# A fused attention, routed-expert and feed-forward kernel: order of loads, first scores and the mask matmuls

## The chip, the core and the metric

The kernel runs on one core of one Trainium2 chip. The metric is the device time of one execution, in microseconds (us); the runs shown are three executions, of which the median counts. One further execution was recorded by the hardware profiler, and all rows of a profile below come from it.

## What is computed

The reference has three stages. The result of each is the input of the next.

```
scores = q k^T / 8, block-causal over blocks of 64      # 4 batches, 8 heads, 576 rows, 64 columns
x   = softmax(scores) v                                 # 2304 tokens x 512
keep = x @ w_skip > 0;  e = argmax(x @ w_gate)          # one of 8 experts for a token that is kept
x[keep] += gate * (relu(x @ w1[e]) @ w2[e])             # w1: 512 x 1024, w2: 1024 x 512 for each expert
h   = x @ w_in;  out = (max(h,0) + alpha*min(h,0)) @ w_out   # 2048 wide
```

The weights w_in and w_out arrive in a 64-bit form, which the kernel decodes on VectorE (DVE) into a high and a low part.

## The kernel before

**Attention.** Two heads make a pair, and there are 16 pairs, numbered p. Each goes through the steps `tr` (q and k are turned on TensorE, tiles psq and psk), `tr_tail` (the last 64 rows, tile pst), `sc` (scores, tile pss, five query blocks i in the order 4, 3, 2, 1, 0), `row_max`, `expo`, `ptr` (the exponentials are turned, tile pspt), `pv` (tile pso), `norm` and `xout`. A table `OFF` of step offsets gives the order in which the steps are recorded, so that one pair's steps mix with its neighbours', and a scheduler then sets each engine's order. q and k are split into high and low float32r parts, and a score is the sum of three products (`PARTS`). The mask is one more small matmul of a tile `top` (a one in two rows) with a tile `neg` (a large negative number), which stands behind the first of the three products (L239). Matmuls of a constant tile (`warm`, tile psw) keep TensorE busy at a few places, eight of them behind the first load.

**Loads.** SyncE (SP) issues nearly all DMAs. A load of 512 KB goes through `bulk`: the load number n waits until load n minus `DEPTH` has landed, and `DEPTH` is 2. This wait stands in SP's own row of instructions, so whatever is behind it waits too. Small DMAs of SP (the lists, the rows of x) are not in that chain but stand in the same row.

**Experts.** The first 32 tokens of each expert are worked on together: `s_x` turns the gathered rows, `s_one(e)` is the product with w1 (tile psh), `s_ht(e)` turns its result (tile hts), `s_two(e)` is the product with w2 (tile psy). `AHEAD` is 3, so `s_one` of experts 0 to 2 runs ahead of the loop over experts. What an expert has beyond 32 tokens is done in `extra(e)`, a block under a condition on a register (L794); with this input it is skipped for experts 0, 1, 5, 6 and 7 and taken for 2, 3 and 4. Where it is skipped, each engine jumps. `level0(e)` gathers rows for it by GpSimd (POOL), two experts ahead. Which rows these are stands in the lists `li`, which SP reads from DRAM after GpSimd has scattered them there (L496); `load_list` issues four reads. Weights lie in three sets of buffers, so `load_w(e + 3)` comes after expert e. The last four pieces of expert 2 (its w2) are loaded where the lists are read, behind them. `dec_in` decodes pieces of w_in (raw tile dr, three buffers) between the experts.

**From experts to feed-forward.** `first_decode` decodes the first two pieces of w_out into the tile xz. `first_window` loads the first 512 rows of x into xz (L890), turns them (L899), adds the last group's result by a product with a selection matrix (L902) and splits them into xs. Then the feed-forward loop (`g1`, `act`, `g2`) runs, during whose first sixteen steps the rest of w_out is decoded.

```
def bulk(out, in_, free_run=False):
    ins = nc.sync.dma_start(out=out, in_=in_).ins
    if not free_run:
        if len(chain) >= DEPTH:
            tc.add_manual_dep(ins, chain[-DEPTH].name, ...)
        chain.append(ins)

load_areg(4); s_x(0); sends[B - 1]()       # sends: the list scatters
for i in range(KX): load_list(i)
load_w(2, range(4, 8))
```

Of the kernel before, what the change touches and what calls it, by code (L numbers as in the profile page):

```python
# [32 lines left out]
DEPTH = 2  # L33
# [14 lines left out]
def tile_kernel(ctx: ExitStack, tc: tile.TileContext, q, k, v, w_skip, w_gate, w1, w2, w_in, w_out, alpha, out):  # L48
# [27 lines left out]
    chain = []  # L76

    def bulk(out, in_, free_run=False):
        ins = nc.sync.dma_start(out=out, in_=in_).ins
        if not free_run:  # L80
            if len(chain) >= DEPTH:
                tc.add_manual_dep(ins, chain[-DEPTH].name, mybir.DependencyInfo(mybir.DependencyClass.Sync, mybir.DependencyReason.DATA), reason="few large loads at a time")
            chain.append(ins)
# [63 lines left out]
    top = acst.tile([128, 128], F32R, name="top")  # L147
    nc.vector.memset(top.bitcast(F32), 0.0)
    for r in (0, 64):
        nc.vector.memset(top[r:r + 1, 0:64].bitcast(F32), 1.0)  # L150
    neg = acst.tile([128, 64], F32R, name="neg")
    nc.vector.memset(neg.bitcast(F32), NEG)
# [33 lines left out]
    def load(p, nm, src):  # L186
        b, h0 = p // NP, p % NP * 2
        a = ld.tile([128, 5, 2, D], F32, tag=nm + "r", name=nm + "r")
        for x in range(2):
            nc.sync.dma_start(out=a[:, 0:4, x, :], in_=src[b, h0 + x, 0:512, :].rearrange("(t p) d -> p t d", p=128))  # L190
        nc.sync.dma_start(out=a[0:64, 4], in_=src[b, h0:h0 + 2, 512:S, :].rearrange("h p d -> p h d"))
        st[p][nm + "r"] = a
# [5 lines left out]
    def tr(p, nm):  # L198
        ps = ps_m.tile([128, 512], F32, tag="m", name="ps" + nm)
        for t in range(4):  # L200
            nc.tensor.transpose(ps[:, t * 128:t * 128 + 128], tok4(p, nm, t), ident)
        for c in "hl":
            st[p][nm + c] = tp.tile([128, 512 if nm == "q" else S], F32R, tag=nm + c, name=nm + c)
        split_qk(nm, *(st[p][nm + c][:, 0:512] for c in "hl"), ps)
# [23 lines left out]
    def sc(p, i):  # L228
        d = st[p]
        ps = d["s", i] = ps_s.tile([128, 2, 512], F32, tag="s", name="pss")  # L230
        if i < 4:
            n = 128 * i + 128
            qc = slice(i * 128, i * 128 + 128)
            for k, (a, b) in enumerate(PARTS):
                for x, hs in enumerate(half):
                    nc.tensor.matmul(ps[:, x, 0:n], d[a][hs, qc], d[b][hs, 0:n], start=(k == 0), stop=(k == 2))  # L236
                if k == 0:
                    for x, hs in enumerate(half):
                        nc.tensor.matmul(ps[:, x, n - 64:n], top[hs], neg[hs], start=False, stop=False)  # L239
        else:  # L240
            for c, o in ((slice(0, 512), ps[:, 0]), (slice(512, S), ps[:, 1, 0:64])):
                for k, (a, b) in enumerate(PARTS):
                    nc.tensor.matmul(o, qd[p % 2][:, int(a == "ql")], d[b][:, c], start=(k == 0), stop=(k == 2))

    def row_max(p, i):
# [5 lines left out]
        else:  # L251
            m = sm.tile([128, 1], F32, tag="m4", name="m4", bufs=2)
            nc.vector.tensor_reduce(out=m, in_=ps.rearrange("p x c -> p (x c)")[:, 0:S], axis=AX.X, op=ALU.max, negate=True)
# [309 lines left out]
    start = {load: WARM}  # L563
# [103 lines left out]
    AHEAD = 3  # L667
# [39 lines left out]
    def s_ht(e):  # L707
        hT = mw.tile([128, 2, 128], F32, tag="hts", name="hts", bufs=1)
        trans(sh[e], hT)
        sh[e] = hT  # L710
# [115 lines left out]
    sends[B - 1]()  # L826
    for i in range(KX):
        load_list(i)
    load_w(2, range(4, 8))
# [14 lines left out]
    s_ht(0)  # L844
    xs = {}
# [41 lines left out]
    def first_window():  # L887
        xz = xzs[0]
        for t in range(4):
            nc.sync.dma_start(out=xz[:, t], in_=xd[t * 128:t * 128 + 128, :])  # L890
# [18 lines left out]
    for e in range(E):  # L909
# [9 lines left out]
        else:  # L919
# [3 lines left out]
            s_ht(e + 1)  # L923
# [144 lines left out]
```

## Time and profile before

| | us |
|---|---|
| median of 3 runs | 860.8 |
| lowest and highest | 858.63, 864.05 |
| profiled execution, its own time | 854.09 |
| span of the profiled execution (first to last instruction) | 852.5 |
| TensorE (PE) busy in the span | 799.0 |
| DVE busy in the span | 458.8 |
| ScalarE (ACT) busy | 299.3 |
| GpSimd (POOL) busy | 162.4 |

Times in rows are us from the span's start. PEld is TensorE's weight load, SPq the queue of SyncE. In a row of the timeline, the bracket gives how long the engine had been idle before it and what ended that. PEclk is the granted TensorE clock: 1.00 is 2.4 GHz, 0.50 is 1.2 GHz. A busy time is a modelled one for matmuls, and a row may merge several instructions (x8).

### The profile page before, as it was taken

The page shows a single profiled execution, that of the slowest core. Times are in us where ns is not written, and L with a number is a line of the kernel's source. Part 1 is how long each engine was busy: PE and PEld are TensorE (multiplying, and loading weights), DVE is VectorE, ACT ScalarE, POOL GpSimd, SP SyncE. Part 2 cuts the span into 40 slices and gives each one's busy share as a digit, 9 for nine tenths or more (in the row PEclk, how much of TensorE's full clock was granted, in tenths as well). Part 3 has the DMA queues.
Part 4 walks back from the last instruction along what each step waited for, and adds up shares of the span by engine and source line. Part 5 has one row for each costly group of instructions (what it writes and reads, how often), then busy time and mean ns, then how long its engine had stood idle before and what let it go on. Part 6 is the DMA issues. An engine that isn't in the chain of part 4 may idle for free.

```text
span 852.5 us, 14562 instructions
## 1 busy us (share of the span) xinstructions
PE 799.0 (94%) x5548; PEld 613.9 (72%) x5548; DVE 458.8 (54%) x951; ACT 299.3 (35%) x779; POOL 162.4 (19%) x204
## 2 busy tenths in 40 slices
PE   7999999999986899998599988999999999999998
PEld 4777777777753665765388666888888888888887
DVE  4576757667657167798579898323222332222232
ACT  3777676766641123112143433211111112111111
POOL 1000110110103122313012211321222212222132
PEclk7999999999998799999799999999999999999999
DMA  6765354464313777877723221100110001000100
GB/s 123 169 197 143 87 147 108 96 159 126 95 36 89 251 254 244 267 254 240 239 101 94 80 83 42 50 0 1 50 50 0 1 26 50 0 1 1 38 13 25
DMA packets 96378, 85.84 MB, mean 101 GB/s; under 512 B 68601, under 2 KB 73913, under 8 KB 96272
## 3 DMA queue, kind: packets, MB, share of 16 engines
q1 hardware_dynamic: 93776, 78.88, 32.1%
q0 software_dynamic: 2496, 5.61, 2.0%
q8 instruction: 59, 0.97, 0.5%
q14 instruction: 47, 0.39, 0.2%
HBM read 73.20 MB, written 11.71 MB: 100 GB/s over the span
## 4 chain that ended last, share of the span: by engine, by line
PE 47%; DVE 9%; DMA 4%; issue 2%; ACT 1%; SPq 0%; DVEq 0%; ACTq 0%
PE psf L970 18%; PE psa L1001 6%; PE psa L1002 6%; PE psa L1011 6%; PE psh L752 4%; PE psy L763 3%; DVE dt L640 2%; DMA w2t<-in_moe_w_dram 1%; DVE dr L644 1%; DVE dt L641 1%; DVE gt L983 1%; DMA w1t<-in_moe_w_dram 1%; PE psh L777 1%; DVE dr L642 1%; DVE dr L638 1%
## 5 line engine op out<-in xcount | busy, mean ns | idle before, releaser
L970 PE MATMUL psf<-xs,whi 128*128 128x512 f32 (+1 forms) x640 | 159.6, 371 | 0.7 <-ACT xs L856 0.7
L987 POOL TENSOR_TENSOR gl<-gt,gh 128x512 fp32r<-128x512 f32 (+1 forms) x80 | 96.0, 1200 | 322.9 <-ACT gh L986 190.5
L986 ACT ACTIVATE gh<-gt 128x512 fp32r<-128x512 f32 (+1 forms) x80 | 47.1, 589 | 264.5 <-PE psa L1002 144.7
L970 PEld LDWEIGHTS psf<-xs,whi 128*128 128x128 f32 x640 | 114.3, 188 | 25.4 <-ACT xs L856 0.9
L982 DVE TENSOR_SCALAR gu<-psf,alf 128x512 f32<-128x512 f32 (+1 forms) x64 | 43.7, 683 | 158.3 <-PE psf L970 158.0
L970 PE MATMUL psf<-xs,wlo 128*128 128x512 f32 (+1 forms) x320 | 80.1, 372 | 0.0
L267 ACT ACTIVATE pe<-pss,mx 128x512 f32<-128x512 f32 (+3 forms) x128 | 66.6, 524 | 14.2 <-DVE mx L250 11.8
L970 PEld LDWEIGHTS psf<-xs,wlo 128*128 128x128 f32 x320 | 56.6, 188 | 11.7
L1001 PE MATMUL psa<-whi,gh 128*128 128x512 f32 x144 | 57.3, 398 | 6.5 <-ACT gh L986 6.5
L250 DVE TENSOR_REDUCE mx<-pss 128x2 f32<-128x1024 f32 (+1 forms) x64 | 52.4, 819 | 19.9 <-PE pss L236 17.3
L275 ACT ACTIVATE pt<-pspt 128x512 f32<-128x512 f32 (+3 forms) x112 | 52.1, 488 | 29.4 <-PE pspt L301 28.7
L1001 PE MATMUL psa<-wkg,gh 128*128 128x512 f32 x144 | 57.2, 397 | 1.7 <-ACT gh L986 1.7
L983 DVE SCALAR_TENSOR_TENSOR gt<-psf,gu 128x512 f32<-128x512 f32 (+1 forms) x80 | 51.0, 637 | 13.9 <-POOL gl L987 8.1
L1002 PE MATMUL psa<-wlo,gh 128*128 128x512 f32 x144 | 56.3, 391 | 0.0
L1002 PE MATMUL psa<-wkg,gh 128*128 128x512 f32 x144 | 56.3, 391 | 0.0
L301 PE MATMUL pspt<-ident,pe 128*128 128x128 f32 x320 | 51.5, 287 | 0.1
L326 PE MATMUL pso<-pt,vr 128*64 128x256 f32 (+1 forms) x384 | 47.5, 352 | 2.3 <-ACT pt L275 2.1
L857 DVE TENSOR_TENSOR xs<-psx,xs 128x512 fp32r<-128x512 f32 x18 | 12.4, 692 | 60.4 <-ACT xs L856 60.4
L326 PEld LDWEIGHTS pso<-pt,vr 128*64 128x64 f32 x384 | 30.1, 136 | 16.9 <-ACT pt L275 7.2
L752 PEld LDWEIGHTS psh<-xT,w1t 128*128 128x128 f32 x320 | 39.5, 205 | 1.5 <-issue 1.0
L752 PE MATMUL psh<-xT,w1t 128*128 128x128 f32 x320 | 40.2, 290 | 0.0
L301 PEld LDWEIGHTS pspt<-ident,pe 128*128 128x128 f32 x320 | 33.8, 141 | 6.7 <-issue 2.2
(231 smaller groups left out, 1374.3 us busy)
## 6 DMA issues: line engine op xcount, KB each, us to landing
w1t<-in_moe_w_dram SPq DMA_DIRECT2D x32, 512.0 KB, 4.5
w2t<-in_moe_w_dram SPq DMA_DIRECT2D x32, 512.0 KB, 4.5
dr<-in_moe_w_in_dram SPq DMA_DIRECT2D x16, 512.0 KB, 5.1
dr<-in_moe_w_out_dram SPq DMA_DIRECT2D x16, 512.0 KB, 3.7
out_dram<-ob SPq DMA_DIRECT2D x18, 256.0 KB, 2.0
qr<-in_q_dram SPq DMA_DIRECT2D x32, 128.0 KB, 4.9
kr<-in_k_dram SPq DMA_DIRECT2D x32, 128.0 KB, 2.6
vr<-in_v_dram SPq DMA_DIRECT2D x32, 128.0 KB, 2.5
```

Source lines behind the costliest of these rows:

```text
L250: nc.vector.tensor_reduce(out=m, in_=ps[:, :, 0:128 * i + 128], axis=AX.X, op=ALU.max, negate=True)
L267: ins = nc.scalar.activation(out=pt[:, x, 0:n], in_=ps[:, x, 0:n], func=AF.Exp, bias=m[:, x:x + 1], scale=1.0, accum_out=d["sum"][:, x * 4 ...
L275: nc.scalar.activation(out=o, in_=a, func=AF.Copy)
L301: nc.tensor.transpose(ps[:, y, j, :], e[:, x, j * 128:j * 128 + 128], ident)
L326: nc.tensor.matmul(d["o"][hs, c0:c0 + n * 128], v5[:, j, x, :], pt[:, x, 2 * j:2 * j + n].rearrange("p n c -> p (n c)"), start=(j == 0), s ...
L752: nc.tensor.matmul(ps[:, f], w[:, kk, c:c + 128], self.xT[:, kk], start=(kk == 0), stop=(kk == 3))
L970: nc.tensor.matmul(ps[:, 0:n], wsp[f // 4 * 4 + kk][a][:, ws], c[:, kk, 0:n], start=(n0 == 0 and kk == 0), stop=(n0 == 2 and kk == 3))
L983: nc.vector.scalar_tensor_tensor(out=t[:, 0:n], in0=ps[:, 0:n], scalar=0.0, in1=u[:, 0:n], op0=ALU.max, op1=ALU.add)
L987: nc.gpsimd.tensor_tensor(out=lo[:, 0:n], in0=t[:, 0:n], in1=hi[:, 0:n].bitcast(F32), op=ALU.subtract)
L1001: nc.tensor.matmul(o, hi[:, ts], whi, start=(f == 0), stop=False)
L1002: nc.tensor.matmul(o, hi[:, ts], wlo, start=False, stop=False)
L1011: nc.tensor.matmul(acc[w, t], lo[:, t * 128:t * 128 + 128], whi, start=False, stop=False)
```

## The change

Eight edits are made at once.

1. `DEPTH` goes from 2 to 3: a 512 KB load waits for the third load before it, not the second.
2. The four w2 loads of expert 2 stand ahead of the four list reads. The first of them waits for the ACT copy that ends `s_x(0)` (`tied`, `last_exp`).
3. `AHEAD` goes from 3 to 2 and hts gets two buffers: `s_one(2)` moves from ahead of the loop into the turn of expert 1, `s_ht(1)` from the turn of expert 0 to ahead of the loop.
4. The rows of `first_window` (xz) are loaded by GpSimd's queue; the loads of w_out behind them stay on SP.
5. k of pair 0 is loaded by ACT's queue.
6. The q transposes of pair 1 wait for the first row maximum of pair 0 (`first`).
7. Five more warm-up matmuls are recorded behind `tr_tail(0)`.
8. `top` and `neg` are bfloat16, and the mask matmuls of a block stand behind its three products, as the last of the sum.

```
-DEPTH = 2
+DEPTH = 3
...
+            if tied[0]:
+                tc.add_manual_dep(ins, tied.pop().name, ..., reason="first rows ahead of the weights")
...
-    top = acst.tile([128, 128], F32R, name="top")
+    top = acst.tile([128, 128], BF16, name="top")
...
-    neg = acst.tile([128, 64], F32R, name="neg")
+    neg = acst.tile([128, 64], BF16, name="neg")
...
+        queue = nc.scalar if p == 0 and nm == "k" else nc.sync
...
-            nc.tensor.transpose(ps[:, t * 128:t * 128 + 128], tok4(p, nm, t), ident)
+            ins = nc.tensor.transpose(ps[:, t * 128:t * 128 + 128], tok4(p, nm, t), ident)
+            if p == 1 and nm == "q" and t == 0:
+                tc.add_manual_dep(ins.ins, st[0]["first"].name, ..., reason="first scores first")
...
-                    nc.tensor.matmul(ps[:, x, 0:n], d[a][hs, qc], d[b][hs, 0:n], start=(k == 0), stop=(k == 2))
-                if k == 0:
-                    for x, hs in enumerate(half):
-                        nc.tensor.matmul(ps[:, x, n - 64:n], top[hs], neg[hs], start=False, stop=False)
+                    nc.tensor.matmul(ps[:, x, 0:n], d[a][hs, qc], d[b][hs, 0:n], start=(k == 0), stop=False)
+            for x, hs in enumerate(half):
+                nc.tensor.matmul(ps[:, x, n - 64:n], top[hs], neg[hs], start=False, stop=True)
...
-    start = {load: WARM}
+    start = {load: WARM, tr_tail: 5}
...
-    AHEAD = 3
+    AHEAD = 2
...
-        hT = mw.tile([128, 2, 128], F32, tag="hts", name="hts", bufs=1)
+        hT = mw.tile([128, 2, 128], F32, tag="hts", name="hts", bufs=2)
...
+    tied[0] = last_exp[0]
+    load_w(2, range(4, 8))
     for i in range(KX):
         load_list(i)
-    load_w(2, range(4, 8))
...
     s_ht(0)
+    s_ht(1)
...
-            nc.sync.dma_start(out=xz[:, t], in_=xd[t * 128:t * 128 + 128, :])
+            nc.gpsimd.dma_start(out=xz[:, t], in_=xd[t * 128:t * 128 + 128, :])
...
-            s_ht(e + 1)
+            if e + 1 < AHEAD - 1:
+                s_ht(e + 2)
+            elif e + 1 >= AHEAD:
+                s_ht(e + 1)
```

TensorE at the start of the program, before. psq with qr is here the turned q of pair 1; pss with qd is the scores of pair 0's block 4, pss with kh and qh those of its block 3.

```order
L221 MATMUL pst<-ident,qr 128x64
L221 MATMUL pst<-ident,kr 128x64
L201 MATMUL psq<-ident,qr 128x128 x4
L243 MATMUL pss<-kh,qd_168 128x512
L243 MATMUL pss<-kl,qd_168 128x512
L236 MATMUL pss<-kh,qh 128x512 x2
L243 MATMUL pss<-kh,qd_168 128x512
L243 MATMUL pss<-kh,qd_168 128x64
L239 MATMUL pss<-neg,top 128x64
```

The same place after the change, from the last products of block 4 on.

```order
L249 MATMUL pss<-kh,qd_168 128x64
L249 MATMUL pss<-kl,qd_168 128x64
L249 MATMUL pss<-kh,qd_168 128x64
L243 MATMUL pss<-kh,qh 128x512 x2
L243 MATMUL pss<-kl,qh 128x512 x2
L243 MATMUL pss<-kh,ql 128x512 x2
L245 LDWEIGHTS top
L245 MATMUL pss<-neg,top 128x64
L245 LDWEIGHTS top
L245 MATMUL pss<-neg,top 128x64
L206 MATMUL psq<-ident,qr 128x128 x4
L292 MATMUL pspt<-ident,p_267 128x128 x4
```

The q transposes of pair 1 stood ahead of the first scores and now stand behind two whole blocks of them; the mask matmuls of block 3 stood inside the sum and now end it. All thirteen warm-up matmuls stand ahead of the first transposes, the five new ones too.

SP where the experts begin, before (li are the lists, w2t the w2 of expert 2).

```order
L679 TENSOR_LOAD cnt
L679 ISA x2
L672 DMA li<-lst 128x8x2 x4
L79 DMA w2t<-in_moe_w_dram 128x2x512 x4
L679 TENSOR_LOAD cnt
L679 ISA x2
```

SP at the same place after the change.

```order
L685 TENSOR_LOAD cnt
L685 ISA x2
L80 DMA w2t<-in_moe_w_dram 128x2x512 x4
L678 DMA li<-lst 128x8x2 x4
L685 TENSOR_LOAD cnt
L685 ISA x2
```

The four weight loads and the four list reads have changed places.

SP at the end of the experts, before (L794 is the end of the last condition, xz the rows of the first window, dr raw pieces of w_out).

```order
L804 UNCONDITIONAL_BRANCH
L794 UNCONDITIONAL_BRANCH
L890 DMA xz<-xd 128x512 x4
L79 DMA dr<-in_moe_w_out_dram 128x1024 x3
L950 DMA xw<-xd 128x512 x4
```

POOL at the same place after the change.

```order
L810 UNCONDITIONAL_BRANCH
L800 ISA
L800 UNCONDITIONAL_BRANCH
L898 DMA xz<-xd 128x512 x4
L736 TENSOR_TENSOR yo<-ys,xgs 128x512
L598 DMA xd<-yo,sid 2305x512
```

The four reads of xz have left SP's row, where the loads of w_out now follow the last branch directly, and stand in POOL's row behind the last branch and ahead of the last group's sum and scatter.

## Rows read from the trace of the kernel before

**Rows 1.** Busy time by stage: PE, PEld, DVE, ACT, POOL, then PEclk, DMA share, GB/s
```profile
12.00:246.00 234.00, 231.04 (x2151) 169.05 (x2151) 148.90 (x418) 161.99 (x502) 18.74 (x39) 0.98 0.51 127
...
392.00:432.00 40.00, 25.67 (x414) 19.72 (x410) 26.96 (x48) 9.59 (x28) 8.37 (x9) 0.83 0.69 221
432.00:532.00 100.00, 91.79 (x395) 72.27 (x396) 89.31 (x148) 39.31 (x68) 21.05 (x15) 1.00 0.24 79
```
**Rows 2.** Timeline of PE, start of pairs 0, 1, 2: start us, us, instruction, idle
```profile
1.26 3.59 PE L62 MATMUL psw<-ones 128*128 128x512 bf16 x8 [1.26 <-DVE ones L128]
...
6.12 0.63 PE L201 MATMUL psk<-ident,kr 128*128 128x128 f32 x4 [0.41 <-DMA kr<-in_k_dram]
...
9.64 1.09 PE L201 MATMUL psq<-ident,qr 128*128 128x128 f32 x4 [2.62 <-DMA qr<-in_q_dram]
11.75 0.77 PE L243 MATMUL pss<-kh,qd 128*128 128x512 f32 x1 [1.02 <-ACT qd L212]
...
28.24 0.48 PE L243 MATMUL pss<-kh,qd 128*128 128x512 f32 x1
...
41.86 0.48 PE L243 MATMUL pss<-kh,qd 128*128 128x512 f32 x1
```
**Rows 3.** Busy time and PEclk in single microseconds near the start
```profile
9.00:10.00 1.00, 0.36 (x2) 0.39 (x3) 0.00 (x0) 0.00 (x0) 0.00 (x0) 0.63 0.45 103
...
22.00:23.00 1.00, 1.00 (x8) 0.88 (x8) 0.27 (x1) 0.34 (x3) 0.00 (x0) 0.54 1.33 226
```
**Rows 4.** Timeline of PE: a mask matmul, and a run of short bf16 matmuls
```profile
43.59 0.19 PE L239 MATMUL pss<-neg,top 64*128 64x64 f32 x2
43.62 0.47 PE L236 MATMUL pss<-kl,qh 64*128 64x512 f32 x2
...
251.01 0.24 PE L445 MATMUL psl<-ohb,ones 128*128 128x32 bf16 x4 [0.78 <-DVE ohb L437]
251.11 0.18 PE L446 MATMUL psl<-ohb,tri 128*128 128x40 bf16 x1
```
**Rows 5.** Timeline of SP, PE and POOL from 268 to 285 us
```profile
268.05 3.10 SPq L672 DMA_DIRECT2D li<-lst  x4
268.28 1.95 PE L719 MATMUL psy<-w2t,hts 128*32 128x128 f32 x34 [1.96 <-PEq L794]
...
271.26 7.18 SPq L79 DMA_DIRECT2D w2t<-in_moe_w_dram  x4
...
279.99 0.09 POOL L65 MEMSET pad<- 1x1 f32 x1 [6.14 <-DMA xg<-xd,li]
...
280.86 3.21 PE L719 MATMUL psy<-w2t,hts 128*32 128x128 f32 x56 [4.47 <-issue]
...
284.94 1.46 PE L687 MATMUL pst<-ident,xg 128*128 128x128 f32 x4 [0.25 <-DMA xg<-xd,li]
```
**Rows 6.** Timeline of SP, POOL, DVE and PE from 391 to 427 us
```profile
391.15 6.60 SPq L79 DMA_DIRECT2D w1t<-in_moe_w_dram  x4
...
407.24 0.96 POOL L589 DMA_INDIRECT xg<-xd,li  x1 [0.77 <-POOL pad L65]
...
410.33 5.32 SPq L79 DMA_DIRECT2D dr<-in_moe_w_out_dram  x3
...
415.36 0.43 DVE L637 TENSOR_SCALAR xz<-dr 128x512 int32<-128x512 int32 x1 [7.08 <-PE psy L719]
...
419.89 1.75 SPq L890 DMA_DIRECT2D xz<-xd  x4
...
422.74 4.01 PE L899 MATMUL psx<-ident,xz 128*128 128x128 f32 x16 [3.70 <-DMA xz<-xd]
...
424.62 0.48 DVE L728 TENSOR_SCALAR ys<-ys,gat 128x512 f32<-128x512 f32 x1
...
426.54 4.96 PE L902 MATMUL psx<-xz,ys 128*128 128x128 f32 x32
```
**Rows 7.** GpSimd's gathers (L589): time from issue to landing
```profile
DMA to landing us min/median/max: 3.4/5.6/7.2
```

More of the change, by code (lines that the diff above doesn't have):

```diff
@@ L76, in tile_kernel @@
     chain = []
+    tied = [None]
     def bulk(out, in_, free_run=False):
@@ L80, in bulk @@
         if not free_run:
+            if tied[0]:
+                tc.add_manual_dep(ins, tied.pop().name, mybir.DependencyInfo(mybir.DependencyClass.Sync, mybir.DependencyReason.DATA), reason="first rows ahead of the weights")
+                tied.append(None)
             if len(chain) >= DEPTH:
@@ L146, in tile_kernel @@
     nc.vector.tensor_scalar(out=tlo, in0=tok, scalar1=63, scalar2=None, op0=ALU.bitwise_and)
-    top = acst.tile([128, 128], F32R, name="top")
-    nc.vector.memset(top.bitcast(F32), 0.0)
+    top = acst.tile([128, 128], BF16, name="top")
+    nc.vector.memset(top, 0.0)
     for r in (0, 64):
-        nc.vector.memset(top[r:r + 1, 0:64].bitcast(F32), 1.0)
-    neg = acst.tile([128, 64], F32R, name="neg")
-    nc.vector.memset(neg.bitcast(F32), NEG)
+        nc.vector.memset(top[r:r + 1, 0:64], 1.0)
+    neg = acst.tile([128, 64], BF16, name="neg")
+    nc.vector.memset(neg, NEG)
     thi = acst.tile([128, 5], F32, name="thi")
@@ L188, in load @@
         a = ld.tile([128, 5, 2, D], F32, tag=nm + "r", name=nm + "r")
+        queue = nc.scalar if p == 0 and nm == "k" else nc.sync
         for x in range(2):
-            nc.sync.dma_start(out=a[:, 0:4, x, :], in_=src[b, h0 + x, 0:512, :].rearrange("(t p) d -> p t d", p=128))
-        nc.sync.dma_start(out=a[0:64, 4], in_=src[b, h0:h0 + 2, 512:S, :].rearrange("h p d -> p h d"))
+            queue.dma_start(out=a[:, 0:4, x, :], in_=src[b, h0 + x, 0:512, :].rearrange("(t p) d -> p t d", p=128))
+        queue.dma_start(out=a[0:64, 4], in_=src[b, h0:h0 + 2, 512:S, :].rearrange("h p d -> p h d"))
         st[p][nm + "r"] = a
@@ L200, in tr @@
         for t in range(4):
-            nc.tensor.transpose(ps[:, t * 128:t * 128 + 128], tok4(p, nm, t), ident)
+            ins = nc.tensor.transpose(ps[:, t * 128:t * 128 + 128], tok4(p, nm, t), ident)
+            if p == 1 and nm == "q" and t == 0:
+                tc.add_manual_dep(ins.ins, st[0]["first"].name, mybir.DependencyInfo(mybir.DependencyClass.Sync, mybir.DependencyReason.DATA), reason="first scores first")
         for c in "hl":
@@ L252, in row_max @@
             m = sm.tile([128, 1], F32, tag="m4", name="m4", bufs=2)
-            nc.vector.tensor_reduce(out=m, in_=ps.rearrange("p x c -> p (x c)")[:, 0:S], axis=AX.X, op=ALU.max, negate=True)
+            d["first"] = nc.vector.tensor_reduce(out=m, in_=ps.rearrange("p x c -> p (x c)")[:, 0:S], axis=AX.X, op=ALU.max, negate=True).ins
         d["m", i] = m
```

## The prediction

> **What bounds the kernel now.** I read the busy shares by stage first, then the timeline of the engine that is full in each stage, then the idle times in the stages where none is full.
>
> Attention, from 12 to 246 us, keeps PE busy for 231.0 of 234 us [rows 1]: only less work on PE, or work at a better clock, shortens it. One pair takes 41.86 − 28.24 = 13.62 us there. The first took 28.24 − 11.75 = 16.49 [rows 2]. The clock explains that: PE idles 2.62 us ahead of the transposes of pair 1 at 9.64, PEclk is 0.63 from 9 to 10 us and still 0.54 from 22 to 23 [rows 2, 3], so most of pair 0 runs near 1.2 GHz instead of 2.4.
>
> Between 392 and 432 us no engine is full: PE has 25.7 us of 40, DVE 27.0, and PEclk is 0.83 [rows 1]. The weights of the last expert come first, then three pieces dr of w_out; SP is held by these until 410.33 + 5.32 = 415.65, and its reads of xz go out only at 419.89. DVE waits 7.08 us for the first piece, PE 3.70 us for xz [rows 6]. From 432 to 532 us DVE is the fuller engine, 89.3 us against 91.8 of PE with its modelled ends [rows 1]; this stage starts when the first window is ready, so an earlier window moves everything behind it. The trace thus offers two places: the first pair and the end of the experts.
>
> **The start (edits 5, 6, 7).** Eight warm-up matmuls take 3.59 us, some of it before their pace settles: 0.43 to 0.45 each. Five more cost 5 × 0.43 = 2.1 us at that pace and half of it, 1.1, at the full clock; I take 1.7. They end at 1.26 + 3.4 + 1.7 = 6.35, where psk started at 6.12, after a wait of 0.41 for k [rows 2]. So ACT's queue for k is worth nothing alone: the warm-up covers k's landing with it or without it. Transposes psk take 0.63, psq of pair 0 as much and the last rows little: about 7.5. Scores came 1.02 us behind the last transposes because of ACT's copies [rows 2]; I allow 1.25, as k's and q's copies are now closer together. That gives the first scores at 8.75 instead of 11.75: −3.0.
>
> The 2.62 us wait for q of pair 1 disappears, for it now stands behind the scores of two blocks. The wait that replaces it, for the first row maximum, has queued behind it on PE only what follows those two blocks, and that has some 4 us of scores as cover; if DVE is late there, it costs a few tenths. What is idle is 1.25 us rather than 2.62, so I expect the clock to stay at 2.4 GHz. Pair 0 then takes somewhat less than 13.62, since no earlier pair's values are mixed into it, and some waits for copies remain: 13.0 against 16.49, −3.5. Together −6.5. If the clock falls all the same, only the −3.0 is left; if the added gaps are longer, it could be zero.
>
> **The mask (edit 8).** There are 64 blocks with two mask matmuls each. Before, the product that follows starts 0.03 us after the two [rows 4]; free of cost after the edit that is 64 × 0.03 = 1.9 us gained. A short bf16 matmul starts 0.10 / 4 = 0.025 us behind another [rows 4]: 128 × 0.025 = 3.2, and against 1.9 that is 1.3 lost. I take 0, in the middle; the row maximum waits for two tiny matmuls more, beside PE's next block.
>
> **Expert 2's weights and the lists (edits 2, 3).** SP issued the list reads at 268.05 for 3.10 us and the w2 loads from 271.26 to 278.44. Expert 2's extra part starts at 284.94 on the landing of its gathered rows, not of w2 [rows 5]. Its w2 is wanted only later, so loading it earlier buys nothing at first; the lists behind four loads of which the fourth waits for the first to land may come up to 4 us later, and with them the gathers. On the other side the loads behind move forward by some of the 7 us. s_one(2) only changes place (1.9 us of matmuls like those at 268.28), s_ht(1) too. I take 0 with −4 and +4 as ends.
>
> **Three loads (edit 1) and xz by GpSimd (edit 4).** From the first w1 issue at 391.15 to the end of the last dr issue at 415.65 stand eleven loads: 24.5 / 10 = 2.45 us each with two in flight [rows 6]. If latency sets the pace, three give two thirds, 1.63; if bandwidth sets it, 2.45 stays (the mean there is 221 GB/s, DMA share 0.69 [rows 1]). I take 1.9. The first dr goes out at 391.15 + 8 × 1.9 = 406.4, lands about 5.5 later (it took 415.36 − 410.33 = 5.0) and is decoded from 412 instead of 415.36. DVE's step L728 behind the decodes comes at 424.62 − 3.4 = 421.3.
>
> The xz reads on POOL wait for its gather at 407.24 (0.96 to issue) to land, 5.6 at the median and 7.2 at most [rows 6, 7], and for two joins of branches: 416. Four issues at the gather's 0.96 bring 420; the last lands some 3 us later, 423, at about the time at which L899 can follow. PE's L902 then starts near 423 instead of 426.54 [rows 6]: −3.5. Less time at half clock gives about 1.5 back, crowding of the DMA engines takes about 1: −4. If the bandwidth bounds and POOL is slow: 0 to +3. If all loads land at 1.63 and PE never slows: −8. In the stretch before, from 304 to 392, a faster stream buys nothing, since the next weights wait for buffers that PE's work frees; the last expert's w1 starts at 391 for that reason.
>
> The row shows DVE decoding in operations of 0.43 us just when POOL would issue. The Trainium skill, "SBUF — State Buffer", section "SBUF: two separate sides", says that a DMA issued from GpSimd has its descriptors written by GpSimd, which is locked out while DVE runs an operation in a 2-port mode. By that rule the xz reads would be late; no row here shows a GpSimd DMA beside decodes. It is the second rival below.
>
> **The sum.** −6.5 + 0 + 0 − 4 = −10.5. The profiled execution took 854.1 (span 852.5 and 1.6 around it), which gives 843.6. The median of the runs is 860.8, 6.7 above it; a time that is compared with this median has to carry this difference, so 860.8 − 10.5 = 850.3, and I predict 850.
>
> **Rivals.** All are given on the median.
>
> *The clock falls anyway.* Thirteen warm-up matmuls, then a gap of 1.25 us and small pieces: PEclk fell to 0.63 behind a gap of 2.62 [rows 2, 3], and nothing shows what 1.25 does. Then the start gives −3, the end −4: 853.8. Chance 0.17.
>
> *GpSimd is late with xz.* DVE's decodes hold the descriptors back. By rows, each of four issues can wait at most for one 0.43 us operation at a time and the stage gains nothing at its end: −6.5 and 0, 854.3. Against it: the gathers of the same queue land in 5.6 us beside DVE work. Chance 0.13.
>
> *Skipped branches get dearer (slower).* Five experts skip their extra part, and each time PE waits for its own instructions to come. The wait at 268.28, before the w2 loads went out, was 1.96; the one at 280.86, with two of them in flight, 4.47 [rows 5]: 2.5 more. If a third load in flight does such a thing at all five branches, 5 × 2.5 = 12.5 are lost. With the start's −6.5 and nothing at the end, this is +6, 867. It decides from 10.5 / 5 = 2.1 us for a branch on. Against it: the later skips already have two loads beside them, and the third adds less than the first two. Chance 0.14; half of it ends above 869.4.
>
> The Trainium skill, "Runtime: NRT & Kernel Launch", section "Instruction fetch mechanics", states that a taken branch to an instruction outside the fetched window forces a DMA fetch before execution goes on. The two waits of 1.96 and 4.47 fit this; that the load beside it lengthens it is this trace's reading alone.
>
> *The earlier weights hold the lists back.* The change puts w2 ahead, but the lists, and with them all gathers, come later, up to 5 us along expert 2's chain, which is bound by the landing of its rows [rows 5]: 855.3. Chance 0.08.
>
> **How the numbers follow.** The forecast has 0.48 (843 to 853 by itself). A measurement of this kernel tells about 1% from no change. Faster than 852.2: 0.46 from the forecast, a third of the first two rivals (0.10): 0.56. Slower than 869.4: half the third rival and 0.02 from chains not seen: 0.09. The rest, 0.35, is within 1%. The range 842 to 864 takes in all but the third rival's upper part and ends below the forecast by the −8 of the last stage and the −1.9 of the mask not adding up together.
>
> **What would show it.** Right: PEclk near 1 from 9 to 23 us, the first scores at 8.75, pair 1's scores about 6.5 us earlier; dr's first decode and L728 some 3.4 us earlier than their places, measured from the last expert's w1 issue; xz landed before PE asks for it. Wrong: PEclk near 0.5 behind the first scores; idle times behind L794's joins over 4 us at each skipped expert; lists later than 271 measured from `s_x(0)`; xz landing behind the decodes, with PE waiting there as before; loads still 2.4 us apart.

## The result and the profile after

Four executions of the changed kernel took 847.12 to 851.27 us, 849.84 at the median, beside 860.59 for four of the kernel before: ratio 0.9893, 95% interval 0.9858 to 0.9928 (an estimate of its own from the executions; the quotient of the two medians is 0.9875). A second comparison later (ten executions against 28) gave 0.9917, 0.9896 to 0.9938. So it is faster by about 1%, 7 to 9 us. Each ratio further below compares a run with executions of the kernel before made beside it, whose medians were 856.1 to 859.7. The execution in the profile took 848.45 us (span 846.9). The recorded one of before took 854.09, so the two traces differ by only 5.6; where the rest is comes out below.

Line numbers in this table are those of the changed kernel.

| milestone on PE, us | before | after | difference |
|---|---|---|---|
| first scores of pair 0 | 11.75 | 9.40 | -2.35 |
| first scores of pair 1 | 28.24 | 21.45 | -6.8 |
| first scores of pair 2 | 41.86 | 35.02 | -6.8 |
| end of attention: first of the last ten products with the gate weights (L416) | 247.19 | 238.62 | -8.6 |
| experts' first rows (L693) | 258.27 | 249.71 | -8.6 |
| gathered rows of expert 2 (L693) | 284.94 | 277.77 | -7.2 |
| first product behind the taken experts (L709) | 392.77 | 387.42 | -5.35 |
| s_two of the last expert (L725) | 417.09 | 414.12 | -3.0 |
| selection product of the first window (L910) | 426.54 | 422.38 | -4.2 |
| first product of feed-forward (L981) | 432.19 | 426.80 | -5.4 |

8.6 us are gained up to 250, 5.6 of them are gone at 414, and 2.4 come back by 427. From there on nothing changes.

Busy time by stage after, which answers to [rows 1] (PE, PEld, DVE, ACT, POOL, then PEclk, DMA share, GB/s):

```profile
12.00:246.00 234.00, 226.35 (x2201) 166.35 (x2201) 153.59 (x446) 163.16 (x513) 19.88 (x41) 1.00 0.51 127
...
392.00:432.00 40.00, 26.22 (x330) 20.77 (x331) 16.55 (x34) 10.23 (x27) 7.35 (x11) 0.87 0.54 183
432.00:532.00 100.00, 92.04 (x397) 72.38 (x396) 87.33 (x143) 38.63 (x66) 23.24 (x17) 1.00 0.25 79
```

Attention ends 8.6 us sooner, so PE's sum in the first row has some of the next stage's idle time in it. Between 392 and 432 PE is no fuller than before. DVE is down from 26.96 to 16.55 us there, but this is work that moved: the last decodes of w_in ended at 379.9 and not at 408.3, and from 246 to 304 us, where DMA moved 236 GB/s in place of 157, DVE was busy for 36.03 us in place of 27.13. Behind 379.9 DVE stood idle for 24.42 us, until w_out's first piece landed (below).

The start, timeline of PE after, which answers to [rows 2] (start us, us, instruction, idle before it):

```profile
1.26 5.27 PE L62 MATMUL psw<-ones 128*128 128x512 bf16 x13 [1.26 <-DVE ones L132]
6.37 0.60 PE L206 MATMUL psq<-ident,qr 128*128 128x128 f32 x4
6.80 0.60 PE L206 MATMUL psk<-ident,kr 128*128 128x128 f32 x4
...
9.40 0.47 PE L249 MATMUL pss<-kh,qd 128*128 128x512 f32 x1 [1.73 <-issue]
...
11.45 0.66 PE L206 MATMUL psq<-ident,qr 128*128 128x128 f32 x4
...
21.45 0.48 PE L249 MATMUL pss<-kh,qd 128*128 128x512 f32 x1
...
35.02 0.48 PE L249 MATMUL pss<-kh,qd 128*128 128x512 f32 x1
```

Ahead of the first scores one idle time is left, 1.73 us, in place of 2.62 and 1.02. The transposes of pair 1's q (11.45) stand behind two blocks of scores. The clock does not fall, as the single microseconds that answer to [rows 3] show (third from the right):

```profile
9.00:10.00 1.00, 0.60 (x3) 0.55 (x4) 0.42 (x3) 0.44 (x2) 0.00 (x0) 1.00 0.48 110
22.00:23.00 1.00, 1.00 (x9) 0.78 (x9) 0.31 (x1) 0.37 (x2) 0.00 (x0) 1.00 0.58 132
```

What held pair 0 back before is seen better on ACT. Timeline of ACT, before:

```profile
10.76 0.60 ACT L212 ACTIVATE qh<-psq 128x512 fp32r<-128x512 f32 x1 [3.28 <-PE psq L201]
11.38 0.22 ACT L212 ACTIVATE qd<-pst 64x64 fp32r<-64x64 f32 x1
```

The copy qd, on which the first scores waited [rows 2], stood in ACT's row behind the copy of pair 1's q, and that waited for PE's transposes at 9.64, and these for the load. After, the same copy of pair 0 comes first and that of pair 1 behind it:

```profile
9.08 0.22 ACT L219 ACTIVATE qd<-pst 64x64 fp32r<-64x64 f32 x1 [0.89 <-DVE qd L221]
...
12.14 0.59 ACT L219 ACTIVATE qh<-psq 128x512 fp32r<-128x512 f32 x1
```

One block of scores at full clock, timeline of PE, before (at the end of attention) and after (in pair 1):

```profile
231.22 0.49 PE L236 MATMUL pss<-kh,qh 64*128 64x512 f32 x2
231.56 0.19 PE L239 MATMUL pss<-neg,top 64*128 64x64 f32 x2
231.59 0.47 PE L236 MATMUL pss<-kl,qh 64*128 64x512 f32 x2
231.90 0.40 PE L236 MATMUL pss<-kh,ql 64*128 64x512 f32 x2
232.23 0.44 PE L326 MATMUL pso<-pt,vr 128*64 128x256 f32 x2
```

```profile
22.85 0.50 PE L243 MATMUL pss<-kh,qh 64*128 64x512 f32 x2
23.19 0.39 PE L243 MATMUL pss<-kl,qh 64*128 64x512 f32 x2
23.42 0.40 PE L243 MATMUL pss<-kh,ql 64*128 64x512 f32 x2
23.66 0.20 PE L245 MATMUL pss<-neg,top 64*128 64x64 bf16 x2
23.79 0.33 PE L206 MATMUL psq<-ident,qr 128*128 128x128 f32 x1
```

Start to start, the block took 1.01 us and takes 0.94 (as does the block at 222.66 us, at the end of attention after). The mask pair itself now costs more (0.13 against 0.03), but the second and third product take 0.23 and 0.24 in place of 0.31 and 0.33.

The beginning of the experts after, which answers to [rows 5] (timelines of SP, POOL and PE):

```profile
250.84 4.18 SPq L80 DMA_DIRECT2D w2t<-in_moe_w_dram  x4
259.89 3.26 SPq L678 DMA_DIRECT2D li<-lst  x4
...
271.76 0.09 POOL L65 MEMSET pad<- 1x1 f32 x1 [5.82 <-DMA xg<-xd,li]
272.57 0.94 POOL L595 DMA_INDIRECT xg<-xd,li  x1 [0.73 <-POOL pad L65]
...
277.77 1.49 PE L693 MATMUL pst<-ident,xg 128*128 128x128 f32 x4 [0.19 <-DMA xg<-xd,li]
```

The w2 loads are out 5 us ahead of the lists, and yet PE gets expert 2's rows at the end of the same chain: list, gather, gather, 5.2 us from the last issue to PE against 4.1 before.

The end of the experts after, which answers to [rows 6] (timelines of SP, DVE, POOL and PE; PEq and ACTq in a bracket are the instruction rows of PE and ACT themselves):

```profile
385.81 4.04 SPq L80 DMA_DIRECT2D w1t<-in_moe_w_dram  x4
...
399.60 13.64 SPq L80 DMA_DIRECT2D dr<-in_moe_w_out_dram  x5
404.32 0.43 DVE L643 TENSOR_SCALAR xz<-dr 128x512 int32<-128x512 int32 x1 [24.42 <-DMA dr<-in_moe_w_out_dram]
...
412.80 0.87 DVE L893 TENSOR_SCALAR xz<-iot,sidf 128x128 f32<-128x128 bf16 x4
413.66 2.25 POOL L898 DMA_DIRECT2D xz<-xd  x4 [10.21 <-PEq L800]
414.12 1.96 PE L725 MATMUL psy<-w2t,hts 128*32 128x128 f32 x64 [1.29 <-ACTq L800]
417.39 0.49 DVE L734 TENSOR_SCALAR ys<-ys,gat 128x512 f32<-128x512 f32 x1 [3.72 <-ACT ys L729]
418.96 3.58 PE L907 MATMUL psx<-ident,xz 128*128 128x128 f32 x16 [2.89 <-DMA xz<-xd]
422.38 3.73 PE L910 MATMUL psx<-xz,ys 128*128 128x128 f32 x32
```

The first decode of w_out comes 18.5 us behind the last expert's w1 issue (24.2 before), and DVE is done before PE needs it. xz is issued at the moment the last branch lets GpSimd through, 0.5 us ahead of PE's s_two, where SP came 2.8 behind it. PE still waits 2.89 us for xz.

### The profile page after: what moved, and what is told of

The parts are those of the page before. It is cut to its first block, busy times and chain, and to the rows that moved or that the text cites. A ratio compares the mean times of both kernels' runs of the same rounds, so it can differ in the third digit from the quotient of the medians.

```text
span 846.9 us, 14577 instructions
## 1 busy us (share of the span) xinstructions
PE 792.0 (94%) x5553; PEld 610.4 (72%) x5553; DVE 458.7 (54%) x951; ACT 298.2 (35%) x779; POOL 165.6 (20%) x208
## 4 chain that ended last, share of the span: by engine, by line
PE 38%; DVE 9%; issue 2%; DMA 1%; ACT 1%; DVEq 0%; ACTq 0%
PE psf L981 18%; PE psa L1012 6%; PE psa L1013 6%; PE psa L1022 6%; DVE dt L646 2%; DVE dr L650 1%; DVE dt L647 1%; DVE gt L994 1%; DVE dr L648 1%; DVE dr L644 1%; DVE wkg L634 1%; DVE dt L645 1%; DVE dt L643 1%; DMA xz<-xd 1%; PE psx L969 1%
## 5 line engine op out<-in xcount | busy, mean ns | idle before, releaser
L981 PE MATMUL psf<-xs,whi 128*128 128x512 f32 (+1 forms) x640 | 159.6, 371 | 0.7 <-ACT xs L864 0.7
L981 PEld LDWEIGHTS psf<-xs,whi 128*128 128x128 f32 x640 | 114.3, 188 | 25.4 <-ACT xs L864 0.9
L981 PE MATMUL psf<-xs,wlo 128*128 128x512 f32 (+1 forms) x320 | 80.1, 372 | 0.0
L981 PEld LDWEIGHTS psf<-xs,wlo 128*128 128x128 f32 x320 | 56.6, 188 | 11.8
L281 ACT ACTIVATE pt<-pspt 128x512 f32<-128x512 f32 (+3 forms) x112 | 51.8, 488 | 30.7 <-PE pspt L307 28.8
L332 PEld LDWEIGHTS pso<-pt,vr 128*64 128x64 f32 x384 | 29.7, 136 | 18.0 <-ACT pt L281 8.3
```

The costliest lines, as they stand in the source:

```text
L281: nc.scalar.activation(out=o, in_=a, func=AF.Copy)
L332: nc.tensor.matmul(d["o"][hs, c0:c0 + n * 128], v5[:, j, x, :], pt[:, x, 2 * j:2 * j + n].rearrange("p n c -> p (n c)"), start=(j == 0), s ...
L981: nc.tensor.matmul(ps[:, 0:n], wsp[f // 4 * 4 + kk][a][:, ws], c[:, kk, 0:n], start=(n0 == 0 and kk == 0), stop=(n0 == 2 and kk == 3))
```

## The experiments

In the texts below the line numbers are those of the changed kernel where a kernel is built on it; rows carry the line numbers of their own run's kernel. "First rows" are the experts' first rows on PE.

**The kernel before again.** No edit. 

> The kernel before, unchanged. Its profiled execution took 854.1 us, its timed ones 858.6 to 864.1, so one trace against one trace shows only 5.6 us of the 10.8 that the medians differ by. Theory: single executions of the same instructions differ by several us, in the stretch of the experts (246 to 432 us), where the time to land of gathers and loads sets the pace; the first pair and attention repeat to 0.2 us: first scores at 11.75, scores of pair 1 at 28.2, first rows of the experts on PE at 258.3, all again, and the feed-forward part as long as before (420 us from its first product). Rival: the first pair itself differs (how long PE idles ahead of the transposes of pair 1, how long the clock stays low), so pair 1's scores move by 1 us or more; then the start's gain is larger on the median than in the two traces.

Ratio 0.9982 (0.9961 to 1.0003); ten executions at 855.5 to 860.3. First scores at 11.72, pair 1's at 27.76; the end of attention at 246.73, 0.5 earlier than in the first trace. The experts' first rows came at 259.7 and not 258.3, the gathered rows of expert 2 28.6 us behind them (26.7 in the first trace), and feed-forward lasted as long to 0.1 us. So the executions differ behind attention: the first trace of before had a short stretch of experts, 173.9 us from first rows to feed-forward's first product, this one 175.7, and later traces with the same experts 176.5 to 179.8. The rival falls but for half a microsecond at the start.

**Start alone.**

```diff
+        queue = nc.scalar if p == 0 and nm == "k" else nc.sync
...
+            if p == 1 and nm == "q" and t == 0:
+                tc.add_manual_dep(ins.ins, st[0]["first"].name, ..., reason="first scores first")
...
-    start = {load: WARM}
+    start = {load: WARM, tr_tail: 5}
```

> The kernel before with edits 5, 6 and 7 alone (k of pair 0 by ACT's queue, q transposes of pair 1 behind the first row maximum, five more warm-up matmuls). Theory: this is the main gain and all of it lasts: scores of pair 1 at 21.4 us instead of 28.2, PEclk 1.00 from 9 to 23 us, and everything behind 6.8 us earlier: ratio 0.992. Rival: part of it is given back, because the experts' stretch waits for loads and gathers that do not come earlier, or because it only trades for another wait: ratio 0.996 or more, with the first product of feed-forward less than 4 us earlier than in the run of the kernel before.

Ratio 0.9922 (0.9893 to 0.9951), eight executions. Pair 1's scores at 20.83, PEclk 1.00 from 9 to 23, end of attention 7.1 earlier. That trace gives 6 us back in the experts (179.8 for that stretch), as the rival has it, but with these instructions unchanged this is the scatter seen above; the timed executions bear the theory out.

**Mask alone.**

```diff
-    top = acst.tile([128, 128], F32R, name="top")
+    top = acst.tile([128, 128], BF16, name="top")
...
-                if k == 0:
-                    for x, hs in enumerate(half):
-                        nc.tensor.matmul(ps[:, x, n - 64:n], top[hs], neg[hs], start=False, stop=False)
+            for x, hs in enumerate(half):
+                nc.tensor.matmul(ps[:, x, n - 64:n], top[hs], neg[hs], start=False, stop=True)
```

> The kernel before with edit 8 alone (bfloat16 mask matmuls behind the three products). Theory: from pair 2 to the end of attention the trace of the changed kernel is 0.12 us shorter for a pair; this comes from the mask, so the pairs' scores come at the same place up to pair 1 (28.1 to 28.3) and the first rows of the experts on PE at 256.4 instead of 258.3: about -1.8 us, ratio 0.998. Rival: the 0.12 us for a pair come from the other order of loads and transposes that the start leaves behind, and the mask costs nothing and gains nothing: 258.2 to 258.4, ratio 1.000.

Ratio 0.9983 (0.9958 to 1.0008): by the timed runs alone this is open. The traces decide: from pair 2's scores to L416 this kernel takes 203.4 us. Four traces with the old mask take 205.3 to 205.7 (before, the first two runs here and the last), nine others with the new mask 203.6 to 203.7. That is -1.6 to -2.2. Type and place were not told apart: the weight load of `top` took 0.19 us at the mean in float32r and 0.09 in bfloat16, so the type may have a part.

**Without the five warm-up matmuls.**

```diff
-    start = {load: WARM, tr_tail: 5}
+    start = {load: WARM}
```

> The changed kernel without edit 7: eight warm-up matmuls, not thirteen. Theory: PE then waits for q and k and for ACT's copies with less work ahead, idles 3 us or more in all between 4.7 and 8.5 us, the granted clock falls to half, and although the first scores come 0.5 to 1 us earlier than 9.4, those of pair 1 come at 24 to 26 us instead of 21.45; PEclk near 0.50 in much of 9 to 22 us; ratio 0.993 to 0.995. Rival: the new order of scores and transposes alone keeps the clock, the five matmuls only delay: first scores near 8.2, pair 1's near 20.2, PEclk 1.00 throughout, ratio 0.987 to 0.988.

Ratio 0.9886 (0.9856 to 0.9916), no slower than with them. Neither text fits whole. The clock falls, as the theory had it, but for 3 us only; windows of single microseconds (PEclk third from the right):

```profile
8.00:9.00 1.00, 0.88 (x5) 0.77 (x5) 0.45 (x2) 0.23 (x1) 0.00 (x0) 0.93 0.84 190
10.00:11.00 1.00, 1.00 (x8) 0.38 (x6) 0.38 (x1) 0.59 (x1) 0.00 (x0) 0.50 0.83 187
12.00:13.00 1.00, 1.00 (x9) 0.80 (x9) 0.56 (x2) 0.68 (x2) 0.00 (x0) 0.87 0.95 13
```

First scores are at 8.12, 1.28 earlier than with the five; the slow microseconds take that back, and pair 1's scores are at 21.40 against 21.45. No gain from edit 7 shows.

**The changed kernel again.** No edit. 

> The changed kernel, unchanged, beside the three that follow. Theory: the start repeats (first scores at 9.4, scores of pair 1 at 21.45, first rows of the experts on PE at 249.7, each within 0.5 us), the experts' stretch does not (first gathered rows of expert 2 on PE 27 to 31 us behind the first rows), and the timed executions lie at 847 to 852: ratio 0.988 to 0.990. Rival: the recorded execution was a lucky one at the start too, and pair 1's scores come at 22.5 or later.

Ratio 0.9917 as told above; ten executions at 847.9 to 853.0. First scores at 8.57, pair 1's at 20.64, both 0.8 us earlier than in the first trace, which is more than the half that the theory allows; the recorded execution was not a lucky one at the start. Gathered rows 29.7 us behind the first rows.

**Depth 2.**

```diff
-DEPTH = 3
+DEPTH = 2
```

> The changed kernel with two large loads at a time again. Theory: the third load buys only the earlier arrival of w_out's first pieces and an earlier free SP at the end of the experts; the first decode of w_out then stands behind the last expert's w1 issue by 24 us again instead of 18.5, and the window is ready 2 to 3 us later: ratio 0.991 to 0.993 (852 to 853.5). Rival: what the third load gains at the end it costs before, by longer landings of gathers and longer waits of PE behind the skipped branches: those waits fall by 3 us or more in sum, and the time stays at 849 to 850, ratio 0.988 to 0.990.

Ratio 0.9938 (0.9906 to 0.9970): the interval takes in the theory's 0.991 to 0.993 and leaves out the rival's 0.988 to 0.990. The last expert's w1 goes out at 390.2 and the first dr at 409.3, 19.1 apart as before, and the first decode comes 25.1 us behind that w1, as the theory had it. But from the last s_two to L910 the trace takes 5.6 us, as with depth 3: with xz on GpSimd, the late SP no longer matters there. The skipped experts' stretch did not get shorter (27.8). Whether the third load gains anything is undecided: against the changed kernel beside it the intervals allow from 1.5 us faster to 5 us slower.

**Lists first.**

```diff
-    tied[0] = last_exp[0]
-    load_w(2, range(4, 8))
     for i in range(KX):
         load_list(i)
+    load_w(2, range(4, 8))
```

> The changed kernel with the list reads ahead of expert 2's w2 loads again (edit 2 undone). Theory: the w2 loads ahead of the lists crowd the list scatters and ACT's and PE's instructions (ACT was idle twice for 3.5 us there), so without them PE gets expert 2's gathered rows about 1.5 us sooner behind the experts' first rows (26 to 28 us instead of 28.1), and the time falls by 1 to 1.5: ratio 0.987 to 0.988. Rival: the loads behind the lists then come 7 us later, land together with the gathers and make these later: rows 29 us or more behind, ratio 0.990 to 0.992.

Ratio 0.9933 (0.9904 to 0.9962), gathered rows 30.7 us behind the first rows: the theory falls, and no cost of edit 2 shows. The rival's later rows do not show its cause either, for with edit 2 they came 27.8 to 32.7 us behind. Whether edit 2 gains the 2 us between the medians is not resolved.

**xz by SP.**

```diff
-            nc.gpsimd.dma_start(out=xz[:, t], in_=xd[t * 128:t * 128 + 128, :])
+            nc.sync.dma_start(out=xz[:, t], in_=xd[t * 128:t * 128 + 128, :])
```

> The changed kernel with the reads of xz issued by SP again (edit 4 undone). Theory: with three loads in flight SP is free by the time the last skipped branch lets all engines through, so SP issues xz at the same moment as GpSimd did, and its reads land 2.9 us behind the first issue as before and not 5.3: PE's L907 starts 1.5 to 2.5 us earlier against its s_two of expert 7, ratio 0.9865 to 0.988. Rival: SP is still held by the loads of w_out, issues xz 3 us or more behind the start of PE's last s_two, and PE waits longer: L907 8 us or more behind that start, instead of 4.8, ratio 0.991 to 0.993.

Ratio 0.9921 (0.9893 to 0.9949), as the changed kernel beside it. Timeline of SP and PE:

```profile
414.43 1.75 SPq L898 DMA_DIRECT2D xz<-xd  x4
416.28 0.85 SPq L80 DMA_DIRECT2D dr<-in_moe_w_out_dram  x2
...
418.26 1.95 PE L725 MATMUL psy<-w2t,hts 128*32 128x128 f32 x64 [1.29 <-ACTq L800]
420.15 1.97 PE L907 MATMUL psx<-ident,xz 128*128 128x128 f32 x16
422.07 3.84 PE L910 MATMUL psx<-xz,ys 128*128 128x128 f32 x32
```

With three loads in flight SP comes 3.8 us ahead of PE's s_two and PE no longer waits for xz, so the rival falls; the ratio of the theory is not reached either. From issue to landing xz takes 3.4 us by SP (3.3 to 3.8 in the other traces that show it), 4.1 to 6.0 by GpSimd (medians of one to four reads). The gain, 3.8 us from s_two to L910 against 4.9 in the run beside it, is too small for the timed runs. Edit 1 with SP takes the old wait away, edit 4 with depth 2 most of it. With both edits PE waited 2.89 us in the first trace of the change, and 0 to 0.9 at that place in the three others, so the 2.89 is not typical.

This trace also shows the clock rival at work in the changed start: behind the same idle time of 1.73 the clock fell.

```profile
10.00:11.00 1.00, 1.00 (x5) 0.79 (x3) 0.19 (x1) 0.00 (x0) 0.00 (x0) 0.50 0.79 177
```

It was back at 13 us, and pair 1's scores came at 22.88: 13.37 us behind the first scores at 9.51, where it is 12.05 at full clock. The price is 1.3 us.

**Start and mask, experts as before** (edits 1 to 4 undone together).

```diff
-DEPTH = 3
+DEPTH = 2
...
-    AHEAD = 2
+    AHEAD = 3
...
```

> The kernel before with edits 5 to 8: start and mask, but depth, order of the lists, AHEAD and the queue of xz as before. From the runs of single edits the start gives a ratio of 0.992 and the mask 0.998, 0.9905 together; the whole change gave 0.9893 and 0.9917. Theory: the four edits to the experts' stretch give nothing in sum (3 to 4 us less in front of the first window, paid by as much behind the skipped branches and at late gathers), so this kernel is as fast as the changed one: ratio 0.989 to 0.992, attention's end 8 to 9.5 us earlier than before, from the experts' first rows to the first product of feed-forward 174 to 180 us. Rival: the four edits are worth their forecast of 4 us: ratio 0.994 to 0.996.

Ratio 0.9905 (0.9874 to 0.9936), median 847.87: as fast as the whole change. The theory stands, and the rival's 0.994 to 0.996 lies outside the interval: in sum edits 1 to 4 give nothing that shows, though against the second comparison of the whole change the intervals leave about 3 us either way. The table has the means of the six traces with the experts as before (before, again, start, mask, this one, edit 6 alone) and of the four with all of edits 1 to 4 (after, again, without warm-up, without edit 6), each stretch between two milestones of PE:

| stretch | experts before | experts changed | difference |
|---|---|---|---|
| first rows to gathered rows of expert 2 | 28.7 | 29.0 | +0.3 |
| to the first product behind the taken experts | 109.0 | 110.3 | +1.3 |
| to the last s_two (three skipped experts) | 25.9 | 27.9 | +2.0 |
| to the selection product L910 | 8.6 | 5.6 | -3.0 |
| to the first product of feed-forward | 5.0 | 4.4 | -0.6 |
| sum | 177.3 (173.9 to 179.8) | 177.3 (176.9 to 178.2) | 0.0 |

The long parts scatter by 2 to 5 us from trace to trace, so each alone is weak; the sum, and the timed runs, agree. Two of the parts also trade: with the experts as before, the way from the last s_two to L910 took 10.6 us where the three skipped experts took 24.1, and 6.7 where they took 28.7. Together these two parts take 34.6 us before and 33.5 after, so the +2.0 and the -3.0 are not two separate effects.

**Without edit 6.**

```diff
-            if p == 1 and nm == "q" and t == 0:
-                tc.add_manual_dep(ins.ins, st[0]["first"].name, ..., reason="first scores first")
```

> The changed kernel without edit 6: the q transposes of pair 1 do not wait for the first row maximum. Theory: this edit is the start's whole gain: without it pair 1's q transposes and ACT's copy of them stand ahead of pair 0's last copies and scores again, both wait for pair 1's q (landed at about 9.6 before), first scores at 11 to 12, the clock stays at half until 20 us or later, scores of pair 1 at 27 to 28.5: ratio 0.997 to 0.999. Rival: the warm-up matmuls and k by ACT's queue carry it: first scores near 10.5, PEclk 1.00 from 11 us on, scores of pair 1 at 23 to 24, ratio 0.993 to 0.994.

Ratio 0.9968 (0.9940 to 0.9996). The old order is back, on ACT (first fence) and PE (second):

```profile
9.11 0.60 ACT L217 ACTIVATE qh<-psq 128x512 fp32r<-128x512 f32 x1 [0.88 <-PE psq L206]
9.73 0.22 ACT L217 ACTIVATE qd<-pst 64x64 fp32r<-64x64 f32 x1
```

```profile
8.42 0.66 PE L206 MATMUL psq<-ident,qr 128*128 128x128 f32 x4 [0.71 <-DVE ql L219]
10.09 0.47 PE L247 MATMUL pss<-kh,qd 128*128 128x512 f32 x1 [1.02 <-ACT qd L217]
...
22.78 0.48 PE L247 MATMUL pss<-kh,qd 128*128 128x512 f32 x1
```

In this execution the rival's picture holds: pair 1's q is there 1.2 us earlier, as SP no longer issues pair 0's k ahead of it, the clock stays at 1.00, pair 1's scores are at 22.78. But it took 849.86 us, the least of twelve; the other eleven lie at 851.9 to 855.9, and their ratio is the theory's. That the clock falls in those is likely and not shown.

**xz by SP and no extra warm-up.** The diffs of two runs above together. 

> The changed kernel with the xz reads on SP and with eight warm-up matmuls (edits 4 and 7 undone): what the runs so far leave as not needed or slower. Theory: xz by SP lands in 3.4 us and not in 4.1 to 6, the window is ready up to 2 us earlier, the five warm-up matmuls are worth nothing: ratio 0.986 to 0.991, faster than the changed kernel by 0 to 2 us. Rival: the edits only help together, ratio 0.992 or more.

Ratio 0.9923 (0.9896 to 0.9951), not faster than the changed kernel, as the rival has it. Pair 1's scores at 19.79 without a fall of the clock, s_two to L910 3.8 us, and 30.9 us for the three skipped experts. No kernel tried here is faster than the changed one beyond the intervals.

**Edit 6 alone.** The dependence of the run without edit 6, added to the kernel before. 

> The kernel before with edit 6 alone: the q transposes of pair 1 wait for the first row maximum of pair 0; k by SP and eight warm-up matmuls as before. Theory: this edit carries the start's gain. PE's last transposes of pair 0 end at 7, ACT's and DVE's copies follow without the copy of pair 1's q between them, first scores at 8.5 to 9.2; whether the clock falls for some us there or not, scores of pair 1 come at 20.5 to 22.5, and the ratio is 0.991 to 0.994, as with all three edits of the start (0.9922). Rival: k's landing and the warm-up matmuls are needed with it: the clock falls and stays low, pair 1's scores come at 24 or later, ratio 0.995 or more.

Ratio 0.9932 (0.9903 to 0.9962), first scores at 8.57, pair 1's at 22.85: the theory, though pair 1 comes a little later than it said: pair 0 took 14.28 us. The clock falls and returns at 16 us:

```profile
9.00:10.00 1.00, 1.00 (x8) 0.85 (x6) 0.23 (x2) 0.00 (x0) 0.00 (x0) 0.72 0.55 126
15.00:16.00 1.00, 1.00 (x6) 0.71 (x4) 0.65 (x1) 0.48 (x2) 0.00 (x0) 0.50 0.19 5
16.00:17.00 1.00, 1.00 (x20) 0.65 (x20) 0.30 (x1) 0.60 (x1) 0.00 (x0) 0.87 0.25 6
```

Even so 5.4 of the start's 6.8 us are there. One edit, the order of pair 1's transposes, carries most of the change's gain.

## Why the prediction came out as it did

The median, 849.84, is where the forecast put it (850), and the direction and the place of the main gain were right. The sum was right by two errors that cancel in part, and by the sample.

- **Start, -6.5 forecast:** -6.8 in the trace, 0.78% or 6.7 us by the timed run of these edits alone. The split was off: first scores at 9.40, not 8.75 (1.73 us idle, not 1.25), pair 0 in 12.05 us, not 13.0. The mechanism was half seen. The text had the wait of PE for pair 1's q, not that ACT's copy of it blocked pair 0's last copies. Whether the warm-up matmuls have the part in holding the clock that it gave them stays open: in the traces with edit 6 the clock fell in one of seven with thirteen of them and in two of three with eight, and no run is slower for having eight. k by ACT's queue does more than forecast ("worth nothing alone"): it brings pair 1's q forward, 1.2 us in the run without edit 6; what that is worth beside edit 6 no run separates.
- **The clock rival (-3 left of the start):** it comes true in three of ten traces with edit 6, but is cheap: pair 0 took 13.29, 13.37 and 14.28 us there against 12.06 at full clock, so the price is 1.2 to 2.2, where its working had 3.5. The low spell lasts 3 to 7 us with scores first, against some 14 before; that this is because pair 0's scores and copies were spread over it is argued.
- **Mask, 0 forecast:** -1.7. This step failed by its choice: the middle of the bounds was taken, and the result lies near the end of -1.9 that [rows 4] gave. The working was wrong as well: the mask pair did not become free, the two products behind it became shorter.
- **Expert 2's weights and lists, 0 forecast:** +0.3 by the traces, and the run with the lists first is no faster. The fourth rival (gathers held back) is not seen.
- **Three loads and xz, -4 forecast:** at their place they give 3.0 + 0.6 = 3.6, as worked out: loads came 1.7 us apart (13.8 us for eight from 385.81 to 399.60; 1.9 forecast), the first decode is early, xz is there sooner. DVE's step behind the decodes (L734) came 31.6 us behind the last expert's w1 issue in place of 33.5, 1.9 earlier and not 3.4, for it now waits for ACT. The 1.5 from the clock and the 1 for crowding in that sum no run separates. What failed is the sentence that a faster stream costs and buys nothing from 304 to 392, and the zero for the skipped branches ahead of the window: +1.3 and +2.0 there, by the means, and the whole term is 0. This would be the third rival in small, at 0.7 us for a branch and not 2.1 and more. But that the traffic of the third load does it is not shown. Over the three skipped experts DMA moved 262 and 267 GB/s in the two traces of the changed kernel and 245 and 239 in those of before; yet two traces with depth 2 took as long at less (start alone 28.7 us at 225 GB/s, depth 2 27.8 at 237), and where the +1.3 stands the traffic fell, from 252 and 247 to 230 and 228. The cause stays open; part of it is the trade told above.
- **The second rival (GpSimd late with xz):** it does not show. GpSimd's reads take 4.1 to 6.0 us from issue to landing, SP's 3.3 to 3.8. In the first trace of the change the decodes had ended (412.80) when GpSimd issued at 413.66, and the one read whose landing is known took 5.2. In five others (again, without warm-up, depth 2, lists first, without edit 6) DVE was still decoding; the four issues stood 0.5 to 0.8 us apart there, 0.5 to 0.6 in the first, and the reads took 4.1 to 6.0. The rule of the Trainium skill, "SBUF — State Buffer", section "SBUF: two separate sides", speaks of DVE operations in a 2-port mode, and whether the decodes run in one no row says; these traces show no delay by it. In the trace of before, too, a gather of GpSimd's went out beside decodes (407.24 [rows 6], decodes until 408.3), which the forecast overlooked.
- **The step from trace to median:** the forecast took 6.7 us between the recorded execution of before and its median as a constant. It is no constant: the recorded execution had the shortest stretch of experts in six traces, 173.9 us where their mean is 177.3, which is 3.4 of the 6.7; the rest no trace accounts for. The median of three, 860.8, was itself high: beside the later runs the kernel before had 856.1 to 859.7. -10.5 was the sum; the parts measured by themselves are -6.8 and -1.7, 8.5, and the two comparisons of the whole change gave 1.07% and 0.83%, 9.2 and 7.1 us.

## What to carry to other kernels

At the start of a kernel, look at every engine's row for work of the next tile that waits for a load and stands ahead of this tile's last steps; moving it behind them was worth most of the gain here, and five more warm-up matmuls gained nothing that shows. Where single executions scatter by several us in one stretch, compare the stretches that repeat to a few tenths by trace and the others by timed runs, and take no constant from one execution to the median. A wait removed at one place of a stretch that is bound by loads, gathers and branches may come back at another: measure from the stretch's first to its last milestone.

## What the runs showed of the hardware that was not expected

The same idle time of 1.73 us on PE ahead of the first scores left the clock at 2.4 GHz in six traces (the change twice, start alone, depth 2, lists first, start and mask) and was followed by 1.2 GHz in one, and how long the low spell lasts differs: about 14 us in three traces with the old order (9.3 to 22.9 in the first), about 7 with edit 6 alone, about 3 in the two others. With eight warm-up matmuls 1.77 us idle was followed by 1.2 GHz in one trace and not in the other. Attention on PE repeats to 0.4 us in over 200, by kernel, while from the experts' first rows to feed-forward the same instructions took 173.9 to 179.8 us. And two small float32r matmuls in the middle of a sum went with 0.08 us more on each of the two product pairs behind them (0.31 and 0.33 us, against 0.23 and 0.24 with the two at the end and in bfloat16), which is more than the pair's own 0.03; whether the place or the type does it no run tells.
